# Attention and expert kernel: the transposed score blocks go to their partitions by way of DRAM

## The chip, the core and the metric

The kernel runs on one core of one Trainium2 chip. The metric is the device time of one execution in microseconds (us), the median of several runs. An engine is named as the profile names it: PE is TensorE (PEld its weight loads), DVE is VectorE, ACT is ScalarE, POOL is GpSimd, SP is SyncE, whose only work here is to issue DMA transfers.

## What is computed

Two blocks run one after the other, all in float32. The first is an attention without softmax over 8 batches of 2496 tokens; its output is multiplied with `u`. The second sends each token to one of 8 experts by a hash of its id and applies the two matrices of that expert.

```python
# u, v: (8, 2496, 256)   z: (8, 2496, 64)
scores = (1 / 2496) * z @ z.T                  # per batch, symmetric
x = u * (maximum(scores, 0) ** 2 @ v)          # (19968, 256) rows
expert = token_ids * 2654435761 % 8
for e in range(8):
    out[expert == e] = maximum(x[expert == e] @ w1[e], 0) @ w2[e]    # F = 1024
```

The scores are symmetric. What is computed for queries i and keys j serves, transposed, for queries j and keys i.

## The kernel before

**Tiles.** The 2496 tokens of a batch are 20 tiles: 19 of 128 tokens and a last one, number `TM` = 19, of 64 (`R`). Four tiles make a group (`G` = 4), five groups a batch (`NG` = 5); the last group has 448 queries, the others 512. A *block* is the 512 x 512 squared scores of one group of keys against one group of queries, kept in SBUF as four tiles `a` of 128 keys each. A 128 x 128 tile splits into *quarters* of 32 (`Q` = 32, `NQ` = 4).

**The order.** The whole program is written out by hand: the loops of Python emit the instructions, and every engine runs its own in the order in which they were emitted. The main loop goes over 40 pairs of batch and group (L651). For one group `g` of queries it runs

- `attend`: for each tile `t` of keys two matmuls (the even and the odd columns of `v`), weights from `v`, moving data the squares of that tile; sums over the tiles in two PSUM banks `acc`. Tiles of the group itself come last, the last three of them (`LATE`) only after the scores of the next group have been emitted;
- `attend_last` (L326): the short tile 19, as two pairs of matmuls of 64 rows each;
- `scores` for the next group (L203): matmuls of `z` against itself into six PSUM buffers, and a Relu into `a`, nearly always on ACT;
- after each step of `attend`: `square` (ACT, in place), `turn_scores` (transposes that are due), and `between` (L595), which counts the step `i`, fetches finished rows, and lets POOL scatter either one column of token numbers to DRAM (`enter`, L550, every fourth step in the middle of the attention) or 128 finished rows (`place_x`, L562).

**Which blocks are computed.** For group `g` only the blocks with keys in groups above `g` and the group's own block are computed (`fresh`). The blocks with keys below `g` are the transposes of earlier ones. They are kept in six buffers `mirror`. A batch has ten such blocks; four of them are made in group 0, three in group 1, two in group 2, one in group 3.

**Turning a block** (`turns_of`, L234). A block is turned in four turns, one for each quarter `c` of the queries. DVE transposes all 32 x 32 squares of that quarter from `a` into a buffer `stage` of 128 x 512 (L241); there are five such buffers (`spool`). The transposed data lie on partition quarters `r` by the key's place in its tile, but must get to the partition quarter `c`. Three of the four pieces go by DMA from SP (L251), 64 KB each in runs of 512 B; the one with `r == c` is already on its partitions and is copied by ACT (L249), in the next step. A `stage` is free again when these four have ended. `turn_now` forces what is still undone before a use. Some 1.2 turns are emitted in each step.

**The own block** (`own_turns`, L255): its lower half is filled in place by 32 to 48 small DVE transposes (L262), which stand behind the turns on DVE. The tiles of the own block that `LATE` uses need them.

**Rows of x** (`gate`, L334). DVE transposes each `acc` into `x_q` (L339, two buffers). Four transfers write it to DRAM (`x_way`, L346), and three steps later one or two read it back row by row into `x_sb` (L349, L351). POOL multiplies by `u` (L354), and the rows wait for `place_x`.

**Semaphores.** Every SP transfer waits on SP for what it needs, and nothing behind it on SP is issued until then.

After the attention come the expert blocks (`run`, L772), which take 512 or 128 tokens each. The change doesn't alter them, apart from the names of the dimensions of their buffers.

## Time and profile before

| what | value |
|---|---|
| median of 3 runs | 2682.76 us (2680.69 to 2684.29) |
| the profiled execution | 2685.0 us |
| its span, first to last instruction | 2683.3 us |
| granted PE clock, mean over the span | 0.996 of full speed |
| attention, up to the first expert matmul | 1560 us of the span |
| DVE: transposes into `stage` (L241) | 320, 218.0 us |
| DVE: transposes inside own blocks (L262) | 1408, 298.8 us |
| SP: transfers out of `stage` (L251) | 960 of 64 or 48 KB, 599 ns each in the median on SP |
| POOL: scatters of token numbers (L550) | 160, 156.3 us |
| all DMA | 357.21 MB, 133 GB/s in the mean |

The busy time of an engine is a sum over the span; the engines run side by side, so these sums don't add up to the span. A DMA that SP issues keeps SP busy only while it is being issued; the transfer itself runs on the DMA engines. The step of PE in a long run of equal matmuls is the distance of their starts, which is shorter than the length shown for one, as they overlap. A float32 matmul shows as two records.

### The profile page before, as it was taken

The numbers are of one execution on the slowest core, as the hardware profiler recorded it, in microseconds if no ns is written. First come the engines' busy times: TensorE is split into PE (matmuls) and PEld (weight loads), VectorE is DVE, ScalarE is ACT, GpSimd is POOL, SyncE is SP. The second block draws the span as 40 slices with busy tenths as digits, with TensorE's granted clock in tenths as the row PEclk, the third lists the DMA queues.
The fourth block names the chain that finished last, engine by engine and source line by source line (L and its number), as shares of the span: only waits on it lengthen the run. The fifth ranks groups of instructions, "written<-read, shape, count | busy, mean of one in ns | idle before, by whom it ended". The sixth has DMA issues, their size and how long they took to land. (4 is left out here: it accounts for less than half of the span.)

```text
span 2683.3 us, 28098 instructions
## 1 busy us (share of the span) xinstructions
PE 2652.4 (99%) x8854; PEld 1534.3 (57%) x8854; DVE 795.7 (30%) x2147; ACT 785.0 (29%) x1592; POOL 608.9 (23%) x671
## 2 busy tenths in 40 slices
PE   9999999999999999999999999999999999999999
PEld 5444444444444444444444457777777777777777
DVE  5634334434334333344344311111111111111110
ACT  7316326324334345245245101111111111111111
POOL 1331332233233233232321121111111111111112
PEclk9999999999999999999999999999999999999999
DMA  5544445545435534534534386666666666666663
GB/s 150 155 119 99 117 109 115 116 105 121 113 99 129 111 102 112 121 98 114 131 97 115 92 204 160 159 158 157 155 154 161 163 164 163 163 164 161 159 156 87
DMA packets 524247, 357.21 MB, mean 133 GB/s; under 512 B 277660, under 2 KB 487085, under 8 KB 524096
## 3 DMA queue, kind: packets, MB, share of 16 engines
q1 hardware_dynamic: 503360, 314.29, 50.1%
q0 software_dynamic: 20736, 41.09, 4.8%
q8 instruction: 72, 1.18, 0.2%
q14 instruction: 79, 0.65, 0.1%
HBM read 229.36 MB, written 67.53 MB: 111 GB/s over the span
## 5 line engine op out<-in xcount | busy, mean ns | idle before, releaser
L323 PE MATMUL acc<-a,v_sb 128*128 128x512 f32 (+1 forms) x1760 | 768.0, 593 | 0.0
L742 PE MATMUL h_ps<-v_sb,m 128*128 128x128 f32 (+1 forms) x2080 | 569.6, 432 | 3.0 <-DVE v_sb L644 1.9
L323 PEld LDWEIGHTS acc<-a,v_sb 128*128 128x128 f32 x1760 | 343.0, 197 | 391.6 <-issue 374.7
L754 PE MATMUL o_ps<-m,hT 128*128 128x256 f32 x2576 | 566.3, 379 | 0.0
L323 PE MATMUL acc<-m,v_sb 128*128 128x512 f32 (+1 forms) x1280 | 529.2, 571 | 5.5 <-DVE x_q L339 4.5
L754 PEld LDWEIGHTS o_ps<-m,hT 128*128 128x128 f32 x2576 | 487.0, 190 | 78.3 <-issue 15.0
L742 PEld LDWEIGHTS h_ps<-v_sb,m 128*128 128x128 f32 x2080 | 318.1, 191 | 238.0 <-issue 231.4
L323 PEld LDWEIGHTS acc<-m,v_sb 128*128 128x128 f32 x1280 | 250.5, 196 | 279.8 <-issue 267.7
L748 DVE TENSOR_SCALAR hT<-h_ps 128x512 f32<-128x512 f32 x161 | 111.4, 692 | 946.3 <-PE h_ps L742 540.6
L218 ACT ACTIVATE a<-s_ps 128x512 f32<-128x512 f32 (+3 forms) x456 | 203.6, 566 | 588.5 <-PE s_ps L210 439.6
L766 POOL DMA_INDIRECT out_dram<-o_sb,idx x157 | 153.6, 979 | 925.0 <-ACT o_sb L761 917.1
L354 POOL TENSOR_TENSOR x_sb<-x_sb,u_sb 128x256 f32<-128x256 f32 (+1 forms) x160 | 111.1, 723 | 989.0 <-DMA x_sb<-x_way 766.1
L262 DVE STREAM_TRANSPOSE a<-a 32x64 f32<-32x64 f32 (+3 forms) x1408 | 298.8, 241 | 20.0 <-ACT a L226 6.4
L249 ACT COPY m<-stage 32x512 f32<-32x512 f32 (+1 forms) x320 | 189.6, 593 | 300.9 <-DVE stage L241 139.7
L241 DVE STREAM_TRANSPOSE stage<-a 128x512 f32<-128x512 f32 x320 | 218.0, 700 | 200.8 <-DMA m<-stage 179.5
L226 ACT ACTIVATE a<-a 128x512 f32<-128x512 f32 (+1 forms) x480 | 236.9, 564 | 2.1
L761 ACT COPY o_sb<-o_ps 128x256 f32<-128x256 f32 x161 | 60.0, 372 | 596.6 <-PE o_ps L754 596.6
L210 PE MATMUL s_ps<-zT 64*128 64x512 f32 (+2 forms) x960 | 207.6, 555 | 16.7 <-ACT a L218 11.3
L339 DVE STREAM_TRANSPOSE x_q<-acc 128x512 f32<-128x512 f32 (+1 forms) x80 | 56.4, 705 | 552.1 <-PE acc L323 501.5
L746 ACT ACTIVATE hT<-h_ps 128x512 f32<-128x512 f32 x161 | 96.1, 597 | 398.9 <-PE h_ps L742 390.7
L210 PEld LDWEIGHTS s_ps<-zT 64*128 64x128 f32 x960 | 118.4, 192 | 123.0 <-issue 75.6
L562 POOL DMA_INDIRECT x_rows<-x_sb,slot_i x160 | 157.7, 986 | 43.2 <-issue 37.2
(93 smaller groups left out, 390.2 us busy)
## 6 DMA issues: line engine op xcount, KB each, us to landing
m<-in_moe_w_dram SPq DMA_DIRECT2D x260, 256.0 KB
m<-in_moe_w_dram SPq DMA_DIRECT2D x65, 1024.0 KB
m<-stage SPq DMA_DIRECT2D x768, 64.0 KB
v_sb<-in_v_dram SPq DMA_DIRECT2D x32, 512.0 KB
u_sb<-in_u_dram SPq DMA_DIRECT2D x32, 512.0 KB
x_way<-x_q SPq DMA_DIRECT2D x128, 128.0 KB
x_sb<-x_way SPq DMA_DIRECT2D x32, 512.0 KB
v_sb<-x_rows SPq DMA_DIRECT2D x128, 128.0 KB
```

The costliest lines, as they stand in the source:

```text
L210: nc.tensor.matmul(ps[:, lo:n], zT[b][h, ts(t, P)], zT[b][h, ds(g * G * P + lo, n - lo)], start=True, stop=True)
L218: nc.scalar.activation(a, ps[:, lo:n], AF.Relu)
L226: nc.scalar.activation(a, a, AF.Square, scale=1.0 / S)
L241: nc.vector.transpose(stage[:].rearrange("p (n q) -> p n q", q=Q), made[key][:].rearrange("p t (s q) -> p (t s) q", q=P)[:, :, ts(c, Q)])
L249: to_copy.append((key, lambda o=o, x=x: nc.scalar.copy(o, x)))
L262: return lambda: nc.vector.transpose(out, in_)
L323: nc.tensor.matmul(acc[h][:, 0:queries(g)], v_sb[b][:, t, h::2], squares(b, g, t), start=(k == 0), stop=(k == TM - 1), skip_group_check=True)
L562: st = nc.gpsimd.indirect_dma_start(out=x_dram[:, :], out_offset=bass.IndirectOffsetOnAxis(ap=slot_i[0:width(c % T), c:c + 1], axis=0), in ...
L742: nc.tensor.matmul(ps[:, ts(i, n)], w1[j][:, c, ts(k * m + i, P)], xT[j][:, :, c, :], start=(c == 0), stop=(c == DP - 1))
L748: nc.vector.tensor_scalar_max(o, ps[:], 0.0)
L754: nc.tensor.matmul(ps[:], hT[j][f][:, ts(t, P)], w2[j][:, f, :], start=(f == 0), stop=(f == FP - 1))
L766: st = nc.gpsimd.indirect_dma_start(out=out[:], out_offset=bass.IndirectOffsetOnAxis(ap=rows, axis=0), in_=o, in_offset=None, bounds_check ...
```

## The change

`stage` is written to DRAM whole, in one transfer a turn, and when all four turns of a block have been written, one transfer reads the block back into its `mirror`. The DRAM tensor `way` has the quarter and the partition in it as its first two dimensions, so the read is 128 rows of 8 KB. There are four such tensors, taken in turn. The read is put into the list `to_fetch` and is issued two steps after the block's last turn, or at once where the block is used earlier. The list `to_copy` and its ACT copies are gone.

The dimensions of `mirror` are now (quarter r, tile i, source tile s, query q) in place of (i, r, s, q), and the columns of `acc` follow: quarter first, then tile. In the last group two of the four quarters have four tiles and two have three, so `squares` gives two parts there, of 256 and 192 columns, and each matmul of that group becomes two. `x_way` has its rows in this order too, and its read is four transfers, one for each quarter of the partitions. The blocks read directly (`a`) are read in runs of 32 columns. `spool` has six buffers for five, `qpool` one for two.

```diff
-    qpool = pool("qpool", 2)
-    spool = pool("spool", 5)
+    qpool = pool("qpool", 1)
+    spool = pool("spool", 6)
...
+    way = [nc.dram_tensor(f"way_{k}", (NQ, Q, NQ, G * G * Q), F32) for k in range(4)]
...
             nc.vector.transpose(stage[:].rearrange("p (n q) -> p n q", q=Q),
                                 made[key][:].rearrange("p t (s q) -> p (t s) q", q=P)[:, :, ts(c, Q)])
-            for r in range(NQ):
-
-                m = len(group(g)) if r * Q < width(group(g)[-1]) else G - 1
-                o = mirror[key][ts(c, Q), 0:m, r].rearrange("p i s q -> p i (s q)")
-                x = stage[ts(r, Q), 0:m * G * Q].rearrange("p (i n) -> p i n", i=m)
-                if r == c:
-                    to_copy.append((key, lambda o=o, x=x: nc.scalar.copy(o, x)))
-                else:
-                    nc.sync.dma_start(o, x)
+            nc.sync.dma_start(ways[key][c].rearrange("j r x -> r j x"), stage[:])
+            if c == NQ - 1:
+                to_fetch.append((i + 2, key, lambda: nc.sync.dma_start(
+                    mirror[key][:].rearrange("p r i s q -> p (r i s q)"), ways[key][:].rearrange("c j r x -> (c j) (r x)"))))
...
         if t in fresh(b, g):
-            a = made[b, g, t // G][:, t % G, :].rearrange("p (n q) -> p n q", q=Q)
+            a = made[b, g, t // G][:, t % G, :].rearrange("p (i r q) -> p r i q", r=NQ, q=Q)
         else:
-            a = mirror[b, t // G, g][:].rearrange("p i r s q -> p s (i r) q")[:, t % G]
-        return a[:, 0:queries(g) // Q]
+            a = mirror[b, t // G, g][:, :, :, t % G, :]
+        parts, c = [], 0
+        for r in ([slice(0, NQ)] if TM not in group(g) else [slice(0, R // Q), slice(R // Q, NQ)]):
+            m = G if r.start < R // Q else G - 1
+            n = (r.stop - r.start) * m * Q
+            parts.append((slice(c, c + n), a[:, r, 0:m]))
+            c += n
+        return parts
...
         for h in halves:
-            nc.tensor.matmul(acc[h][:, 0:queries(g)], v_sb[b][:, t, h::2], squares(b, g, t),
-                             start=(k == 0), stop=(k == TM - 1), skip_group_check=True)
+            for cols, a in squares(b, g, t):
+                nc.tensor.matmul(acc[h][:, cols], v_sb[b][:, t, h::2], a,
+                                 start=(k == 0 and cols.start == 0), stop=(k == TM - 1), skip_group_check=True)
...
-        def fetch():
-            nc.sync.dma_start(xs[:, 0:m], o[0:m].rearrange("i j p d -> (j p) i d"))
-            if m < G:
-                nc.sync.dma_start(xs[0:R, m], o[m, 0:R // Q].rearrange("j p d -> (j p) d"))
+        def rows_of_x():
+            c = 0
+            for r in range(NQ):
+                m = G if r * Q < width(group(g)[-1]) else G - 1
+                nc.sync.dma_start(xs[ts(r, Q), 0:m], o[c:c + m].rearrange("i p d -> p i d"))
+                c += m
...
-        if to_fetch and to_fetch[0][0] <= i:
-            to_fetch.pop(0)[1]()
+        fetch(lambda e: e[0] <= i)
```

More of the change, by code (lines that the diff above doesn't have):

```diff
@@ L81 @@
     xpool = pool("xpool", 3)
-    qpool = pool("qpool", 2)
-    spool = pool("spool", 5)
+    qpool = pool("qpool", 1)
+    spool = pool("spool", 6)
     x_dram = nc.dram_tensor("x_rows", (NS * P, D), F32)
-    x_way = [nc.dram_tensor(f"x_way_{k}", (G, NQ, Q, D), F32) for k in range(2)]
+    way = [nc.dram_tensor(f"way_{k}", (NQ, Q, NQ, G * G * Q), F32) for k in range(4)]
+    x_way = [nc.dram_tensor(f"x_way_{k}", (G * NQ, Q, D), F32) for k in range(2)]
     slot_dram = nc.dram_tensor("slot_tokens", (P * NS,), I32)
@@ L122 @@
     uf, vf, zf = (x.rearrange("b s d -> (b s) d") for x in (u, v, z))
-    zn, zT, v_sb, u_sb, x_q, made, mirror, to_square, to_turn, to_fetch, gated = {}, {}, {}, {}, {}, {}, {}, [], [], [], []
+    zn, zT, v_sb, u_sb, x_q, made, mirror, ways, to_square, to_turn, to_fetch, gated = {}, {}, {}, {}, {}, {}, {}, {}, [], [], [], []
     def load_z(b):
@@ L239, in turn @@
                 mirror[key] = mirrors.pop(0)
+                ways[key] = way[len(ways) % len(way)]
             stage = spool.tile([P, G * G * Q], F32, name="stage")
@@ L275, in own_turns @@
                         yield move(tiles[ds(h * R + c * Q, Q), 3, 0:3, ts(r, Q)], tiles[i, 0:3, 3, ts(c, Q)])
-    to_copy = []
     share = 0
@@ L282, in turn_scores @@
         nonlocal share
-        copy_turned(to_copy[:])
         share += 1.2 * steps
@@ L296, in turn, with fetch @@
         e[1]()
-    def copy_turned(those):
-        for e in those:
-            to_copy.remove(e)
-            e[1]()
+    def fetch(due):
+        for e in [e for e in to_fetch if due(e)]:
+            to_fetch.remove(e)
+            e[2]()
     def turn_now(key):
@@ L305, in turn_now @@
             turn(e)
-        copy_turned([e for e in to_copy if e[0] == key])
+        fetch(lambda e: e[1] == key)
     def squares(b, g, t):
         if t in fresh(b, g):
-            a = made[b, g, t // G][:, t % G, :].rearrange("p (n q) -> p n q", q=Q)
+            a = made[b, g, t // G][:, t % G, :].rearrange("p (i r q) -> p r i q", r=NQ, q=Q)
         else:
-            a = mirror[b, t // G, g][:].rearrange("p i r s q -> p s (i r) q")[:, t % G]
-        return a[:, 0:queries(g) // Q]
+            a = mirror[b, t // G, g][:, :, :, t % G, :]
[6 more added lines that the diff above has]
+        return parts
     def attend(b, g, k, acc, halves):
@@ L322, in attend @@
         for h in halves:
-            nc.tensor.matmul(acc[h][:, 0:queries(g)], v_sb[b][:, t, h::2], squares(b, g, t),
-                             start=(k == 0), stop=(k == TM - 1), skip_group_check=True)
+            for cols, a in squares(b, g, t):
+                nc.tensor.matmul(acc[h][:, cols], v_sb[b][:, t, h::2], a,
+                                 start=(k == 0 and cols.start == 0), stop=(k == TM - 1), skip_group_check=True)
     def attend_last(b, g, acc):
         turn_now((b, TM // G, g))
-        for h in range(2):
-            rows = ds(h * R, R)
-            nc.tensor.matmul(acc[h][:, 0:queries(g)], v_sb[b][rows, TM, h::2], squares(b, g, TM)[rows],
-                             start=False, stop=False, skip_group_check=True)
+        for cols, a in squares(b, g, TM):
+            for h in range(2):
+                rows = ds(h * R, R)
+                nc.tensor.matmul(acc[h][:, cols], v_sb[b][rows, TM, h::2], a[rows],
+                                 start=False, stop=False, skip_group_check=True)
     def gate(b, g, h, acc):
@@ L345, in gate @@
         for a in range(NQ):
-            nc.sync.dma_start(o[:].rearrange("i j p d -> p (i j) d")[:, 0:n, ts(a, D // NQ)], x[ts(a, Q), 0:n])
-        m = len(whole(g))
-        def fetch():
-            nc.sync.dma_start(xs[:, 0:m], o[0:m].rearrange("i j p d -> (j p) i d"))
-            if m < G:
-                nc.sync.dma_start(xs[0:R, m], o[m, 0:R // Q].rearrange("j p d -> (j p) d"))
+            nc.sync.dma_start(o[:].rearrange("n p d -> p n d")[:, 0:n, ts(a, D // NQ)], x[ts(a, Q), 0:n])
+        def rows_of_x():
[4 more added lines that the diff above has]
+                c += m
             for k, t in enumerate(group(g)):
@@ L355, in fetch @@
                 gated.append((b * T + t, y))
-        to_fetch.append((i + 3, fetch))
+        to_fetch.append((i + 3, None, rows_of_x))
     idx = const.tile([P, NS], I32)
@@ L407, in places @@
             total, rank = counts[:, 0], counts[:, 1]
-            room = sorting[:].rearrange("p i r s q -> p (i r s q)")
+            room = sorting[:].rearrange("p r i s q -> p (r i s q)")
             upto = room[:, 0:E * C].rearrange("p (e c) -> p e c", e=E)
@@ L629, in load_w @@
     def load_w(j, k):
-        w1[j] = w_buf[2 * k][:].rearrange("p i r s q -> p (i r s q)").rearrange("p (h f) -> p h f", h=DP)
-        w2[j] = w_buf[2 * k + 1][:].rearrange("p i r s q -> p (i r s q)").rearrange("p (c d) -> p c d", c=FP)
+        w1[j] = w_buf[2 * k][:].rearrange("p r i s q -> p (r i s q)").rearrange("p (h f) -> p h f", h=DP)
+        w2[j] = w_buf[2 * k + 1][:].rearrange("p r i s q -> p (r i s q)").rearrange("p (c d) -> p c d", c=FP)
         e = nc.sync.value_load(eb_i[0:1, j:j + 1], min_val=0, max_val=E - 1)
@@ L646 @@
     mpool = pool("mirror", 1)
-    mirrors = [mpool.tile([P, G, NQ, G, Q], F32, name=f"m_{k}") for k in range(NG * NG // 4)]
+    mirrors = [mpool.tile([P, NQ, G, G, Q], F32, name=f"m_{k}") for k in range(NG * NG // 4)]
     sorting = mirrors.pop()
@@ L714 @@
     assert not to_turn and next(place, None) is None and i > SORT + 4 * C
-    for _, f in to_fetch:
-        f()
+    fetch(lambda e: True)
     while gated:
```

## The prediction, made before the changed kernel had run

> **What bounds the kernel now.** I read the page's busy shares first, then the timeline of TensorE at the seams between query groups, then SP, DVE and POOL at one of these seams, then the DMA queues.

> ```profile
> PE 2652.4 (99%) x8854; PEld 1534.3 (57%) x8854; DVE 795.7 (30%) x2147; ACT 785.0 (29%) x1592; POOL 608.9 (23%) x671
> ...
> L249 ACT COPY m<-stage 32x512 f32<-32x512 f32 (+1 forms) x320 | 189.6, 593 | 300.9 <-DVE stage L241 139.7
> ```

> TensorE is busy for 99% of the span. ScalarE is not the bound, so the 189.6 us of copies that go (L249) are worth only what they hold up. Work of TensorE that is added costs its whole length; a stall of TensorE costs its whole length too.

> The timeline shows where it is not fed. Call A0 to A4 the attention stages of one batch's five groups and S1 the scores between A0 and A1 (L331 and L210). Batch 1 first, then batch 7, the last:

> ```profile
> 237.12 1.14 PE L331 MATMUL acc<-a,v_sb 64*128 64x512 f32 x4
> 238.09 2.74 PE L210 MATMUL s_ps<-zT 64*128 64x512 f32 x12
> 242.88 5.86 PE L210 MATMUL s_ps<-zT 64*128 64x512 f32 x20 [2.05 <-ACT a L218]
> 248.68 1.56 PE L323 MATMUL acc<-a,v_sb 128*128 128x512 f32 x3
> ...
> 1407.70 1.14 PE L331 MATMUL acc<-a,v_sb 64*128 64x512 f32 x4
> 1408.67 6.60 PE L210 MATMUL s_ps<-zT 64*128 64x512 f32 x32
> 1415.20 1.13 PE L323 MATMUL acc<-a,v_sb 128*128 128x512 f32 x2
> ```

> From L331 to the next L323, S1 takes 11.6 us in batch 1 and 7.5 in batch 7. Summed over the eight batches, S1 is 23.9 us above 7.5 each, and S2 (5.6 at best) 11.9 above: 36 us, the only sizable slack. The other stages repeat to 0.1 us, but for 7.5 us in all at the starts of A4.

> ```profile
> 237.62 0.98 POOL L550 DMA_INDIRECT slot_tokens<-token,addr  x1 [0.30 <-issue]
> 238.91 0.98 POOL L550 DMA_INDIRECT slot_tokens<-token,addr  x1 [0.30 <-issue]
> ...
> 213.48 7.81 SPq L251 DMA_DIRECT2D m<-stage  x12
> 221.46 0.46 SPq L349 DMA_DIRECT2D x_sb<-x_way  x1
> ...
> 216.93 0.71 DVE L241 STREAM_TRANSPOSE stage<-a 128x512 f32<-128x512 f32 x1 [3.52 <-DMA m<-stage]
> ...
> 236.71 3.80 DVE L262 STREAM_TRANSPOSE a<-a 32x64 f32<-32x64 f32 x17
> ```

> The slow S1 and S2 are those in which POOL's token scatters (L550) run into the scores; batch 7 has none and no stall. They come in a burst after x_sb lands, and x_sb is late because its fetch (L349) queues on SP behind turns at 1.95 us each (three transfers). DVE is paced by the same transfers: it waits for a free `stage`, and its last turns of the own block (L262 x17) end at 240.5, before A1 needs them (A0 began at 204.9, so A1 could begin at 244.6). That leaves DVE about 4 us of room.

> [...] Every SP transfer of the kernel before in this stage has 32, 64 or 128 rows outermost[...]. [...] SP's longest wait for `x_way` is 2.8 us. [...] the granted clock falls to a half for 3.4 us after the 2.05 us stall above (the mean of that stretch is 0.96), and so I count 1.7 us for each long stall.

> **The change part by part.**

> *Matmuls of the last group.* 304 matmuls of 448 columns (L323; two records each, 608) become 256 + 192, and 16 pairs of half height (L331) become 32.

> ```profile
> 1530.35 24.22 PE L323 MATMUL acc<-m,v_sb 128*128 128x448 f32 x64
> ...
> 1573.81 13.98 PE L754 MATMUL o_ps<-m,hT 128*128 128x256 f32 x64
> 1587.62 3.73 PE L742 MATMUL h_ps<-v_sb,m 128*128 128x128 f32 x32
> ```

> A run of n is n-1 steps and one length (541, 379 and 275 ns), so a step is 376 ns for 448 columns, 216 for 256, 111.5 for 128; 192 lie between the last two, 164. So 380 against 376: 608 x 4 ns = 2.4 us. A half-height pair costs some 0.1 us beyond its columns, 16 more pairs 1.7 us. Together +4 us. If the weight load (197 ns) bound the 192 columns it would be 608 x 33 = 20 us more; the row of 128 columns at 111.5 ns with a load each excludes that. Reading `a` in runs of 32 costs nothing: L323 on `m` does so already and takes 592 ns against 596.

> *ScalarE copies.* 320 copies go, 189.6 us off an engine that TensorE seldom waits for. Nothing by itself.

> *SP.* A turn issues one transfer instead of three (1.95 us to some 0.6), plus a quarter of a read; the `x_sb` fetch has four issues instead of one or two (+0.8 us). By itself this brings x_sb and L550 forward by about 6 us and takes them out of S1 and S2: up to -36 us.

> *The write of a turn.* Its target is `ways[key][c].rearrange("j r x -> r j x")`: the slowest dimension is r, of 4. The source has 128 partitions. [...] 64 KB on each of four DMA engines[...]. This is the step that decides. How long 64 KB take on one engine is not in the trace; two bounds. [...] Above, the rate of the stores that the trace has:

> ```profile
> q0 software_dynamic: 20736, 41.09, 4.8%
> ```

> 4.8% of 16 x 2683.3 us for 41.09 MB is 19.9 GB/s, 3.3 us. I take 2.9. [...]

> *What it does to DVE.* There are now 6 `stage` buffers, so turn n waits until turn n-6 has landed. The 16 turns of A0 and 12 of A1 come at 1.5 us each and are served at 2.9 plus the rest. Load of these four engines from the start of A0 until the last turn of A1 (the 28th, freed by the 22nd) may start, estimates from packet counts at the queue's rates: 22 writes x 2.9 = 63.8; 5 mirror reads of 1 MB, 64 KB an engine, 2.6 each = 13; the rows through `x_way` twice, write 2.3 and read 1.3, = 7.2; u and the scattered rows 2.8. Sum 86.8. Add 5 until the first turn is there (208.35 + 0.71 against 204.9), 2.6 where SP waits for the writes of the last key and has nothing else in the rings[...]: 96.4. Then the turn and some 20 own turns behind it, 5.6: DVE is done at 102.0. TensorE needs that block at the start of A2, without stalls at 39.7 (A0 and S1: 32.2 + 7.5) + 38.4 (A1 and S2: 32.8 + 5.6) = 78.1. So 24 us of stall a batch, some 7 of them already at A1 (10 writes: DVE done at 46.7 against 39.7). A2 has 8 turns and A3 4, so the queue drains there and in A4: 40 writes x 2.9 = 116 us and 10 reads = 26 fit into 193 us a batch, so nothing carries over. 8 x 24 = 192 us.

> *The reads into the mirrors.* SP waits for the landing of four writes; behind it stand the next turns' writes and the x_sb fetch. Their consumers are 15 or more steps of 1.7 us away, so TensorE does not wait for a mirror itself.

> *x_q with one buffer.* Its next use is 35 us later. Nothing. *End of attention:* +1 us, the chain x_way, x_sb, scatter, load to the first expert blocks.

> Sum: 2685.0 (the profiled execution; its span 2683.3) + 192 + 16 stalls x 1.7 = 27 for the clock + 4 + 1 - 36 = 2873. The first batch has less to move (no rows of a batch before, some 4 us), and the median of the runs is 2 us lower: **2865**.

> **The rivals.**
> *B, the writes spread over all 16 engines (faster).* Then a write is 0.7 us, DVE is never late, SP's load falls, and the 36 us of S1 and S2 go but for 2 or 3: 2682.8 - 34 + 5 = **2654**. For it: the stall stands and falls with L550. Against: the outermost dimension of 4. It decides if writes land in under some 1.7 us.
> *C, four engines, but fast.* [...] 2685 + 88 + 20 + 5 - 36 = 2762, **2760**.
> *D, spread, and the stall of S1 and S2 stays* because L550 only meets other loads: only +5, **2688**, no gain. The L331 to L323 times would show it.
> That the copies might not really go is no rival: L249 is gone from the program.

> **How the numbers follow.** Forecast A 0.62, C 0.20, B 0.14, D 0.04. A's own range is 2790 (2.5 us a write) to 2960 (3.3 us: 9 more a batch). The range 2690 to 2960 leaves out B, D and A's upper tail, under 2 in 10. A measurement here can tell about 0.2%, 5 us. Faster: B, 0.14. Same: part of D, 0.02. Slower: 0.84.

> **What would show it.** Right: DVE's L241 waiting for `way<-stage` in A0 and A1, by 2.5 to 3.3 us a turn; TensorE waiting at the starts of A1 and A2 on DVE's L259 (the own turns), 7 and 17 us; more half-clock stretches; L323 of 256 and 192 columns stepping at 216 and 164. Wrong: turns at 1.5 us with `stage` free, S1 at 7.5 us in every batch, a span near 2655.

## The result, and the profile after

| | kernel before | changed kernel |
|---|---|---|
| median | 2681.73 us (2679.57 to 2684.29, 4 runs) | 2864.2 us (2857.06 to 2878.41, 4 runs) |
| ratio | | 1.0693, 95% interval 1.0673 to 1.0713 |
| profiled execution, span | 2685.0, 2683.3 us | 2857.06, 2855.4 us |
| granted PE clock, mean | 0.996 | 0.972 |
| attention, up to the first expert matmul | 1560 us | 1732 us |

The change made the kernel 6.9% slower; the forecast was 2865 us. The profile of the changed kernel first, its busy shares and three of the groups (busy us and mean ns of one, then idle time before them and what ended most of it); the last line is the transposes into `stage` in the kernel before:

```profile
PE 2688.1 (94%) x9494; PEld 1646.0 (58%) x9494; DVE 791.5 (28%) x2147; ACT 588.5 (21%) x1272; POOL 609.0 (21%) x671
...
L327 PE MATMUL acc<-a,v_sb 128*128 128x512 f32 (+2 forms) x1856 | 805.6, 592 | 124.8 <-DVE a L259 100.7
...
L327 PE MATMUL acc<-m,v_sb 128*128 128x512 f32 (+2 forms) x1792 | 534.7, 458 | 18.4 <-DMA m<-way 13.7
...
L243 DVE STREAM_TRANSPOSE stage<-a 128x512 f32<-128x512 f32 x320 | 219.3, 701 | 520.6 <-DMA way<-stage 493.5
...
L241 DVE STREAM_TRANSPOSE stage<-a 128x512 f32<-128x512 f32 x320 | 218.0, 700 | 200.8 <-DMA m<-stage 179.5
```

ACT is rid of its copies (785.0 to 588.5 us of busy time), and PE has fallen from 99% to 94% of the span. The third group and the first are one chain: DVE waits 493.5 us for a `stage` whose write hasn't landed (179.5 us for the three transfers of before); its own-block transposes (L259), which stand behind the turns, come late; TensorE waits 100.7 us for them. The second group is a wait that the prediction had excluded: TensorE waits 13.7 us for a mirror.

The timeline of PE shows the two seams of batch 3, S1 from the first L336 and S2 from the second (the first line is the start of A0; the bracket is the idle time before the line and what ended it):

```profile
666.25 6.53 PE L327 MATMUL acc<-a,v_sb 128*128 128x256 f32 x28
...
700.15 1.14 PE L336 MATMUL acc<-a,v_sb 64*128 64x512 f32 x4
701.12 6.17 PE L211 MATMUL s_ps<-zT 64*128 64x512 f32 x26
...
714.46 7.61 PE L327 MATMUL acc<-a,v_sb 128*128 128x512 f32 x12 [3.34 <-DVE a L259]
...
749.47 1.14 PE L336 MATMUL acc<-a,v_sb 64*128 64x512 f32 x4
750.44 4.68 PE L211 MATMUL s_ps<-zT 64*128 64x512 f32 x24
763.49 4.85 PE L327 MATMUL acc<-a,v_sb 128*128 128x512 f32 x7 [8.38 <-DVE a L259]
```

S1 takes 14.3 us against the 7.5 of an undisturbed one, S2 14.0 against 5.6. DVE in the same stretch:

```profile
674.07 3.63 DVE L243 STREAM_TRANSPOSE stage<-a 128x512 f32<-128x512 f32 x6
683.78 0.71 DVE L243 STREAM_TRANSPOSE stage<-a 128x512 f32<-128x512 f32 x1 [6.08 <-DMA way<-stage]
686.38 0.71 DVE L243 STREAM_TRANSPOSE stage<-a 128x512 f32<-128x512 f32 x1 [1.89 <-DMA way<-stage]
688.92 0.71 DVE L243 STREAM_TRANSPOSE stage<-a 128x512 f32<-128x512 f32 x1 [1.83 <-DMA way<-stage]
...
758.26 0.71 DVE L243 STREAM_TRANSPOSE stage<-a 128x512 f32<-128x512 f32 x1 [3.23 <-DMA way<-stage]
759.00 4.43 DVE L259 STREAM_TRANSPOSE a<-a 32x128 f32<-32x128 f32 x20
```

Six turns fill the six buffers within 3.6 us. From then on a turn starts when a write has landed, at best 2.6 us after the one before it (686.38 - 683.78, 688.92 - 686.38), though it takes 0.71; up to 758.26, with the reads of blocks and the rows of x between the writes, it is 3.7 us in the mean of 20. The last own turn ends at 763.43, and TensorE goes on at 763.49.

For all the kernels below I took the same measure from the timeline of PE: the length of each stage in every batch, from the first L327 (L323 before) to L336 (L331) for A0 to A4 and from there to the next L327 for the scores, less the shortest length that any of the kernels shows for it (A0 32.2, S1 7.5, A1 to A3 32.8, S2 5.6, S3 3.9, S4 2.0, A4 29.4, the scores after A4 8.9; the A0 of batch 0, which is shorter, counts as 0). Sums over eight batches, us:

| kernel | A0 | S1 | A1 | S2 | A2 | S3, A3 | from A4 | all |
|---|---|---|---|---|---|---|---|---|
| before | 0 | 23.9 | 0 | 11.9 | 2.1 | 0.4 | 7.4 | 45.7 |
| changed | 19.7 | 56.1 | 17.2 | 61.6 | 15.4 | 20.9 | 20.3 | 211.2 |
| e1, four writes | 0 | 8.6 | 0 | 1.1 | 2.5 | 0.4 | 11.4 | 24.0 |
| e2, two engines | 21.1 | 255.1 | 15.9 | 294.4 | 17.8 | 199.1 | 193.8 | 997.1 |
| e3, rows outermost | 0 | 0 | 0 | 0 | 0 | 0 | 3.9 | 3.9 |
| e4, before, scatters moved | 0 | 0.7 | 0 | 0 | 0 | 0.5 | 26.5 | 27.7 |
| e5, changed, pools of before | 19.3 | 81.7 | 18.3 | 76.6 | 18.8 | 10.6 | 3.5 | 228.8 |
| e6, changed, scatters moved | 0 | 61.8 | 19.5 | 59.9 | 16.5 | 18.8 | 101.6 | 278.1 |
| e7, changed, five stages | 0 | 90.0 | 16.3 | 78.1 | 18.7 | 12.2 | 2.0 | 217.3 |

What the changed kernel lost lies in the attention: 211.2 - 45.7 = 165.5 us; from there to the end it takes 7.5 us more (1135.3 for 1127.8), as the first expert matmul waits 7.4 us for its rows of x (DVE, L649). Together 173.0 us, against 172.1 between the spans.

### The profile page after: what moved, and what is told of

It is laid out like the page before. It is cut to its first block, busy times and chain, and to the rows that moved or that the text cites. A ratio compares the mean times of both kernels' runs of the same rounds, so it can differ in the third digit from the quotient of the medians.

```text
span 2855.4 us, 28325 instructions
## 1 busy us (share of the span) xinstructions
PE 2688.1 (94%) x9494; PEld 1646.0 (58%) x9494; DVE 791.5 (28%) x2147; ACT 588.5 (21%) x1272; POOL 609.0 (21%) x671
## 3 DMA queue, kind: packets, MB, share of 16 engines
q0 software_dynamic: 20736, 41.09, 5.1%
## 5 line engine op out<-in xcount | busy, mean ns | idle before, releaser
L327 PE MATMUL acc<-a,v_sb 128*128 128x512 f32 (+2 forms) x1856 | 805.6, 592 | 124.8 <-DVE a L259 100.7
L327 PEld LDWEIGHTS acc<-a,v_sb 128*128 128x128 f32 x1856 | 370.8, 204 | 527.5 <-issue 394.1
L327 PE MATMUL acc<-m,v_sb 128*128 128x512 f32 (+2 forms) x1792 | 534.7, 458 | 18.4 <-DMA m<-way 13.7
L758 PEld LDWEIGHTS o_ps<-m,hT 128*128 128x128 f32 x2576 | 487.0, 190 | 78.1 <-issue 14.8
L327 PEld LDWEIGHTS acc<-m,v_sb 128*128 128x128 f32 x1792 | 337.1, 198 | 215.6 <-issue 179.2
L243 DVE STREAM_TRANSPOSE stage<-a 128x512 f32<-128x512 f32 x320 | 219.3, 701 | 520.6 <-DMA way<-stage 493.5
L360 POOL TENSOR_TENSOR x_sb<-x_sb,u_sb 128x256 f32<-128x256 f32 (+1 forms) x160 | 111.5, 727 | 1148.5 <-DMA x_sb<-x_way 1069.7
L259 DVE STREAM_TRANSPOSE a<-a 32x64 f32<-32x64 f32 (+3 forms) x1408 | 298.2, 241 | 14.2 <-ACT a L227 0.2
L227 ACT ACTIVATE a<-a 128x512 f32<-128x512 f32 (+1 forms) x480 | 227.9, 615 | 0.0
L211 PE MATMUL s_ps<-zT 64*128 64x512 f32 (+2 forms) x960 | 198.6, 538 | 8.5 <-issue 6.5
L556 POOL DMA_INDIRECT slot_tokens<-token,addr x160 | 156.3, 977 | 48.6 <-issue 48.6
```

The lines of the kernel that those rows point to most:

```text
L211: nc.tensor.matmul(ps[:, lo:n], zT[b][h, ts(t, P)], zT[b][h, ds(g * G * P + lo, n - lo)], start=True, stop=True)
L227: nc.scalar.activation(a, a, AF.Square, scale=1.0 / S)
L243: nc.vector.transpose(stage[:].rearrange("p (n q) -> p n q", q=Q), made[key][:].rearrange("p t (s q) -> p (t s) q", q=P)[:, :, ts(c, Q)])
L259: return lambda: nc.vector.transpose(out, in_)
L327: nc.tensor.matmul(acc[h][:, cols], v_sb[b][:, t, h::2], a, start=(k == 0 and cols.start == 0), stop=(k == TM - 1), skip_group_check=True)
L360: nc.gpsimd.tensor_mul(y, y, u_sb[b, g][0:width(t), k, :])
```

## The experiments

Measured again beside e1 to e6, the kernel before took 2677 to 2678 us.

### The four engines: e1, e2, e3

The write of a turn has r, of 4, as the slowest dimension of its target. e1 cuts it into four writes with 32 rows outermost; nothing else changes.

```diff
-            nc.sync.dma_start(ways[key][c].rearrange("j r x -> r j x"), stage[:])
+            for r in range(NQ):
+                nc.sync.dma_start(ways[key][c][:, r], stage[ts(r, Q)])
```

> Undoes one thing of the changed kernel: a turn is written by four transfers of 32 rows each in place of one whose outermost dimension is 4. Same bytes, same rows of 2 KB, same tensor, same read. The theory (the write ran on 4 DMA engines, 2.7 us a turn, and DVE waited for stage): [...] DVE's wait for stage falls from 493 us to under 200, the waits of TensorE for the own turns (100.7 us) are gone, and SP's four issues a turn (some 2 us) set the pace as in the kernel before: 2660 to 2720 us. The rival (the detour through DRAM itself, its volume and landing time): 2830 us or more.

Measured: 2661.82 us (2656.86 to 2665.37), ratio 0.9939 (0.9922 to 0.9957). Same bytes, same buffers, same rows of 2 KB, and the loss is gone. In its view of waits DVE still waits for `stage`, 224.5 us where under 200 were expected, but TensorE no longer for DVE (us in total, times, longest):

```profile
DVE stage L243 <- DMA way<-stage: 224.5, 120, 7.7
...
PE acc L328 <- DVE a L260: 0.7, 1, 0.7
```

e2 goes the other way: two writes a turn, each with two rows outermost.

```diff
-            nc.sync.dma_start(ways[key][c].rearrange("j r x -> r j x"), stage[:])
+            for h in range(2):
+                nc.sync.dma_start(ways[key][c][:, ts(h, 2)].rearrange("j r x -> r j x"), stage[ts(h, R)])
```

> The suspected cost doubled: a turn is written by two transfers whose outermost dimension is 2, [...] 128 KB an engine and turn, 64 rows of 2 KB at 84 ns = 5.4 us a turn. Same bytes. The theory: 40 turns x 5.4 = 215 us, with the mirror reads (26) and the rest (some 25) 266 us a batch on these two engines against 193 us of work: about 8 x 70 = 560 us over the kernel before, 3150 to 3400 us. The rival (volume or landing time): two transfers in place of one change little, 2840 to 2900 us.

Measured: 3647.66 us (3644.97 to 3656.24), ratio 1.3634 (1.361 to 1.3659). The direction is the theory's, the size is more than it gave: the time is outside the range expected. DVE's timeline, with the buffers full:

```profile
358.49 0.71 DVE L243 STREAM_TRANSPOSE stage<-a 128x512 f32<-128x512 f32 x1 [4.47 <-DMA way<-stage]
363.61 0.71 DVE L243 STREAM_TRANSPOSE stage<-a 128x512 f32<-128x512 f32 x1 [4.41 <-DMA way<-stage]
...
368.75 0.71 DVE L243 STREAM_TRANSPOSE stage<-a 128x512 f32<-128x512 f32 x1 [3.81 <-DMA way<-stage]
```

5.1 us a turn, twice the 2.6 with four rows outermost. The packets in the traces point to two DMA engines for a write of two rows and four for one of four. In the attention of these kernels the packets of 2 KB are those of the writes alone (128 a turn, 40960 in the changed kernel). While any is under way there are 2.0 at once in the mean in e2 (at most three for 99.8% of that time), 3.3 in the changed kernel (at most five for 99.5%), and 8.5 in e1. A packet took 84 ns in the median in the changed kernel, so the 128 of a turn would take 2.7 us four at a time and 5.4 two at a time, an estimate beside the 2.6 and 5.1 measured. On which engine a packet ran the traces don't show: "four engines" and "two engines" stand for these counts.

Why e2 lost 970 us and not the 560 of its expectation is shown in part. The expectation had counted that the queue doesn't drain (266 us of load for 193 us of work a batch), but a batch now takes 314 us in the mean. It had not counted that the mirrors come late too:

```profile
PE acc L328 <- DVE a L260: 512.9, 16, 40.1
PE acc L328 <- issue: 216.4, 9, 39.6
PE acc L328 <- DMA m<-way: 166.4, 8, 22.9
```

e3 keeps one write a turn and turns `way` around, so that the write has 128 rows outermost and the permutation is done by the reads, one for each quarter of the partitions.

```diff
-    way = [nc.dram_tensor(f"way_{k}", (NQ, Q, NQ, G * G * Q), F32) for k in range(4)]
+    way = [nc.dram_tensor(f"way_{k}", (NQ, NQ, Q, G * G * Q), F32) for k in range(4)]
...
-            nc.sync.dma_start(ways[key][c].rearrange("j r x -> r j x"), stage[:])
+            nc.sync.dma_start(ways[key][c].rearrange("r j x -> (r j) x"), stage[:])
...
-                to_fetch.append((i + 2, key, lambda: nc.sync.dma_start(
-                    mirror[key][:].rearrange("p r i s q -> p (r i s q)"), ways[key][:].rearrange("c j r x -> (c j) (r x)"))))
+                to_fetch.append((i + 2, key, lambda: [nc.sync.dma_start(
+                    mirror[key][ts(k, Q)].rearrange("p r i s q -> p r (i s q)"), ways[key][k].rearrange("r j x -> j r x")) for k in range(NQ)]))
```

> The changed kernel with the way tensor as (c, r, j, x): a turn is written by one transfer of 128 rows, and a block is read back by four of 32 partitions with rows of 2 KB. [...] Same bytes; 8 issues a block on SP for 5. The theory: no wait of DVE of note; SP's load is below that of the kernel before, the x rows come some 6 us earlier, the token scatters leave S1 and S2, which take 7.5 and 5.6 us: 2645 to 2670 us. If the scatters' overlap was not what held S1 and S2 up: about 2690. The rival (the detour itself): 2800 or more.

Measured: 2642.24 us (2638.59 to 2642.57), ratio 0.9866 (0.9849 to 0.9882): 1.3% faster than the kernel before, 3 us below the range expected. DVE's wait for `stage` is down to 71.6 us. Its busy shares and the seam of batch 1 in its timeline:

```profile
PE 2630.8 (100%) x9494; PEld 1630.4 (62%) x9494; DVE 790.9 (30%) x2147; ACT 584.8 (22%) x1272; POOL 608.1 (23%) x671
```

```profile
235.41 1.14 PE L336 MATMUL acc<-a,v_sb 64*128 64x512 f32 x4
236.38 6.60 PE L211 MATMUL s_ps<-zT 64*128 64x512 f32 x32
242.91 2.42 PE L327 MATMUL acc<-a,v_sb 128*128 128x512 f32 x5
```

7.5 us, without a gap, and so in all eight batches. POOL's burst of token scatters in this batch ends at 234.5, before S1 begins. In e1, where a turn issues four writes on SP for one, three scatters still fall at batch 1's S1, which takes 1.9 us longer there.

### The scatters: e4, e6

e4 is the kernel before with the token scatters (L550) in groups 2, 3 and 4 alone, so that none can run into S1 and S2.

```diff
-        elif i % 4 == 0 and i < SORT + 4 * C:
+        elif entered < C and (i % 3 < 2 if i // 20 % 5 == 3 else i // 20 % 5 > 1 and i % 4 == 0):
...
-            enter((i - SORT) // 4)
+            enter(entered)
+            entered += 1
```

> The kernel before with one thing moved: the scatters of token numbers (L550) are emitted in the groups 2, 3 and 4 alone, so that none runs in S1 or S2. If these scatters are what holds S1 and S2 up: S1 is 7.5 and S2 5.6 us in every batch, 36 us less, 2640 to 2655 us. If SP's backlog of turns or the loads of u and v do it: S1 and S2 unchanged, 2675 to 2690 us.

Measured: 2663.87 us (2659.08 to 2664.47), ratio 0.9945 (0.9928 to 0.9961). S1 and S2 fall from 35.8 us to 0.7, so the scatters are what these stages lost: in the kernel before 12 of them start in S1 and 19 in S2, none here. (The scatters of finished rows, L562, take the steps that are left and shift a little, but none starts in S1 or S2 in either kernel.) But A4, where many of them now are, rises from 7.4 to 26.5, and the time misses the range expected. The cost moved with its cause. PE and DVE in one such A4 (POOL issues scatters, nearly all L550, at a step of 1.28 us up to 942.3):

```profile
938.80 21.54 PE L323 MATMUL acc<-m,v_sb 128*128 128x448 f32 x49 [3.18 <-DVE x_q L339]
...
938.03 0.72 DVE L339 STREAM_TRANSPOSE x_q<-acc 128x512 f32<-128x512 f32 x1 [3.73 <-remote]
938.78 3.02 DVE L262 STREAM_TRANSPOSE a<-a 32x96 f32<-32x96 f32 x16
942.19 0.27 DVE L262 STREAM_TRANSPOSE a<-a 32x96 f32<-32x96 f32 x1 [0.39 <-issue]
943.59 0.33 DVE L262 STREAM_TRANSPOSE a<-a 32x64 f32<-32x64 f32 x2 [1.13 <-DMA x_way<-x_q]
945.00 0.33 DVE L262 STREAM_TRANSPOSE a<-a 32x64 f32<-32x64 f32 x2 [1.08 <-issue]
```

TensorE loses 3.18 us because DVE, which frees its `acc`, starts late at 938.03. Later small transposes that otherwise run 0.2 us apart start only every 1.40 us for a while, mostly with nothing that the profile could name as their releaser. (The wait for `x_way<-x_q` at 943.59 can't be told from this: it ends at the same step.)

e6 makes the same edit in the changed kernel.

> The changed kernel with POOL's token scatters (L550) in groups 2, 3 and 4 only, as in e4_scatters_moved. Theory (the 20 us that the starts of A0 lost in the changed kernel belong to the scatters, which come there by way of the late x_sb; the waits of S1 and S2 belong to the four-engine writes): A0's excess falls below 5 us, S1 and S2 keep 90 us or more, A4 rises by up to 20; 2845 to 2870 us. Rival 1 (A0's excess belongs to the four-engine queue): A0's stays at 15 to 20 us. Rival 2 (the waits at S1 and S2 are the scatters' too): S1 and S2 fall by half or more, below 2800 us.

Measured: 2922.14 us (2915.4 to 2924.45), ratio 1.0909 (1.0885 to 1.0932). A0's 19.7 us go to 0: they were the scatters'. S1 and S2 keep 121.7 us against 117.7: these are the writes'. Both rivals fall. The time is outside the range expected, since from A4 on 101.6 us are lost where up to 40 were expected: the last mirror is late there (below), and on top of it PE starts single matmuls at the same step of 1.40 us:

```profile
442.27 0.38 PE L327 MATMUL acc<-m,v_sb 128*128 128x256 f32 x1 [1.35 <-issue]
443.67 0.32 PE L327 MATMUL acc<-m,v_sb 128*128 128x192 f32 x1 [1.02 <-issue]
445.08 0.32 PE L327 MATMUL acc<-m,v_sb 128*128 128x192 f32 x1 [1.09 <-issue]
...
448.58 0.79 PE L327 MATMUL acc<-m,v_sb 128*128 128x256 f32 x1 [0.82 <-issue]
449.98 0.68 PE L327 MATMUL acc<-m,v_sb 128*128 128x192 f32 x1 [0.61 <-issue]
```

The clock takes its part as well: in this A4, from 418.63 to 460.15, its mean is 0.88, some 5 us of the 12 lost there.

### The waits at A4: e5, e7

In the changed kernel TensorE waits for a mirror in A4. SP and PE in batch 1:

```profile
396.12 0.33 SPq L247 DMA_DIRECT2D m<-way  x1
...
399.25 2.60 SPq L147 DMA_DIRECT2D zn<-in_z_dram  x1
...
412.86 1.73 SPq L356 DMA_DIRECT2D x_sb<-x_way  x4
414.69 3.07 SPq L245 DMA_DIRECT2D way<-stage  x4
417.81 2.64 SPq L121 DMA_DIRECT2D v_sb<-in_v_dram  x1
432.09 0.70 SPq L247 DMA_DIRECT2D m<-way  x1
```

```profile
415.58 18.32 PE L327 MATMUL acc<-m,v_sb 128*128 128x256 f32 x96
437.33 2.98 PE L327 MATMUL acc<-m,v_sb 128*128 128x256 f32 x14 [3.43 <-DMA m<-way]
```

The four writes of the batch's last block are issued only at 414.69, though DVE had turned it by 388.2. SP stood until 396.12 for the landing that the read of the block before waits for, and from 399.25 to 412.7 it issued the loads of `z` for the next batch, then the fetch of `x_sb`. After the four writes it stands until they have landed, to 432.09, before it issues the read, and the mirror is there 5 us later, 3.4 us after TensorE wanted it. e5 asks whether the pools have a share in it: it gives `x_q` its second buffer back and, for lack of room, takes the sixth `stage` away.

```diff
-    qpool = pool("qpool", 1)
-    spool = pool("spool", 6)
+    qpool = pool("qpool", 2)
+    spool = pool("spool", 5)
```

> The changed kernel with the pools of before: stage in five buffers, x_q in two. Theory (the four-engine queue sets the end of DVE's turns, and x_q with one buffer costs nothing): one more write, 2.7 us, must have landed before the last turn of A1 starts, so 8 x 2.7 = 22 us longer than the changed kernel, 2870 to 2900 us; the starts of A0 and A4 keep their waits, 20 us each in the sum over the batches. Rival (the waits at A0 and A4 that were not predicted come from x_q's one buffer, which lets DVE reach the own turns late): these 40 us go and the time falls to 2830 to 2850 us in spite of the buffer lost.

Measured: 2865.79 us (2862.41 to 2870.08), ratio 1.0699 (1.068 to 1.0718). Neither came out. S1 and S2 lose 40.6 us more, 5 a batch where I had put 2.7, and A4 loses 16.8 less, as the rival had it; the whole is the same as the changed kernel's within the intervals. e7 takes only the sixth `stage` away (`spool` 5, `x_q` one).

> The changed kernel with stage in five buffers and x_q in one: it differs from e5_pools_back by x_q alone, from the changed kernel by one stage. Theory (x_q with one buffer costs nothing; the buffer of stage lost moves the stall from A4 to S1 and S2, as in e5_pools_back): A0 to S2 lose 190 to 200 us over the clean lengths, as in e5_pools_back (196), A4 3 to 6, 2860 to 2875 us. Rival (x_q's one buffer is what made A4 wait in the changed kernel, 20 us): A4 loses 15 to 25 us here too and the time is 2880 us or more.

Measured: 2854.82 us (2854.66 to 2859.54), 5 us below the range expected. From A4 on it loses 2.0 us with one `x_q`, so the rival falls, as far as kernels on two chips can be compared: a single `x_q` by itself does not make A4 wait. What the buffer of `stage` does is to shift the wait: in batch 1 of e5 SP issues the four writes at 414.91, within 0.3 us of the changed kernel, but A4 begins at 413.89 instead of 410.31, since TensorE has waited longer before, and so the mirror is in time. A0 to S2 lose 184 us, 6 short of the range expected, with nothing lost in A0. Beside e7, on another chip, the kernel before took 2638.3 us (2637.67 to 2639.39), 40 us less than in all others, so that its ratio of 1.0827 (1.0808 to 1.0845) can't be set beside e5's.

### The same kernels on one chip: e8 to e11

The 2638 us raise a question about e3: is its gain worth anything on that chip? Four kernels were run again, unchanged.

> The kernel before, unchanged. In the call of e7_five_stages it took 2638.3 us, in those of e1 to e6 2677 to 2678. Theory: the 40 us between them are its waits in S1 and S2 (36 us in the profile of before), that is, how much the token scatters hold up differs from chip to chip; the rest is the same on all. Then the tally of its stages gives 0 to 10 us above the clean lengths where it takes about 2638, and 36 to 46 where it takes about 2678. Rival: the chip is faster throughout (clean stages shorter by 1.5%, A1 at 32.3 us for 32.82).

> The changed kernel, unchanged, on the chip of this call. Theory: the stall in S1 and S2 belongs to the four-engine writes and doesn't depend on the chip: A0 to S2 lose 140 to 160 us, 2835 to 2870 us whatever the kernel before takes; where the kernel before takes 2638, A0 alone loses nothing. Rival: it keeps its ratio of 1.069 to the kernel before, 2820 us where that takes 2638.

> e3_rows_outermost, unchanged, on the chip of this call. Theory (it is within 4 us of the clean stage lengths already): 2637 to 2645 us on any chip. So where the kernel before takes 2638 us it is no faster, ratio 1.000 to 1.003; where that takes 2678, 0.985 to 0.989. Rival: the gain is of the copies and transfers saved and holds on any chip: ratio 0.987 in both cases.

> e5_pools_back, unchanged, on the chip of this call, to be read against e9 (one stage more, one x_q less) and, if the chip is that of e7, against e7_five_stages (x_q alone). Theory: the end of DVE's turns is set by the four engines: A0 to S2 lose 185 to 200 us here against 140 to 160 in e9, A4 0 to 5 against 10 to 20; x_q's second buffer is worth less than 8 us. Rival: x_q's second buffer is worth 15 us or more (2840 us or less where e7 took 2855).

Measured, with the kernel before at 2677.63 us beside them: before 2677.37 us (ratio 1.0003, 0.999 to 1.0016), changed 2861.02 (1.0683, 1.0654 to 1.0711), rows outermost 2642.36 (0.9865, 0.9848 to 0.9882), pools of before 2865.67 (1.07, 1.0681 to 1.0719). The stages of e8 lose 41.4 us in all, 33.9 of them in S1 and S2, those of e10 2.3. So e3's gain is repeated, but this was not the chip of e7. What can be said of that one: it is not faster throughout, since the undisturbed stages of e7 are as long as those of e5 (A0 32.21, A3 32.82, A4 29.57 us in both). A0 of e7 lost nothing, where A0 of e5 lost 19.3 and of e11 21.7, as if scatters cost less on it. The profiled kernel before, 2683.3 us, would take 2637.6 without the 45.7 us of the table, about what it took there; and e3's 2642 us on other chips are no less. So e3 would probably gain nothing on that chip. This is not shown: neither e3 nor a profile of the kernel before was taken on it.

e9 beside e11 confirms e5: A0 to S2 lose 151.6 and 196.3 us, from A4 on 26.2 (10 to 20 were expected) and 3.6, and the times are 4.7 us apart. The effect of `x_q` alone was not measured on one chip.

## Why the prediction was right

The mechanism was right. That the total is within 1 us (2865 for 2864.2) is luck: the terms erred in both directions, and the last step of the sum, 2873 less 4 and less 2, gives 2867. On the profiled executions: predicted 192 + 27 + 4 + 1 - 36 = +188. Measured, from the table: 154.6 (A0 to S2) + 15.4 (A2) + 20.9 (S3, A3) + 20.3 (from A4) + 7.5 (start of the experts) - 45.7 (what the kernel before lost) = +173.

- **The write of a turn: right.** That an outermost dimension of 4 means four engines was my assumption; no trace of before showed it. The packets of the changed kernel agree with it (3.3 at once in the mean, at most five for 99.5% of the time), and so do the steps of 2.6 us there and 5.1 in e2. The 2.9 us of a write measured 2.6 (DVE's step; a 2 KB packet took 84 ns in the median, and 32 x 84 = 2.7 us are 64 KB).
- **The stall of DVE: right, 24 us a batch measured 19.3** (A0 to S2, 154.6 us over eight batches, against 192; 17.7 a batch where no scatters add to it, e6). In the batch shown above DVE is done 763.43 - 666.25 = 97.2 us after the start of A0, where I had 102.0 against TensorE's 78.1. A write shorter by 0.3 us is enough for that (22 x 0.3 = 6.6); the other terms were not measured one by one. The 96.4 us of the prediction hold an allowance for the last landing that no trace of before showed by itself; for SP's transfers there is one number here, with the transfer in it: POOL starts on its rows of x at 660.55, 2.6 us after SP has issued the last of their four reads. S1 waits 7.0 us a batch in the mean (7 predicted), S2 7.7 (17 predicted), because the rest of DVE's lateness had been used up before: by A0's own waits and by the half clock of A1.
- **The clock: mis-sized by counting twice.** 16 stalls x 1.7 = 27 us were added. After S2 that is right in size (A2 15.4 us for 8 x 1.7 = 13.6), and it is the clock: in batch 3 A1 takes 35.01 us at a mean clock of 0.94 and A2 34.39 at 0.95, without a gap in either. In A1 17.2 us are lost too, but they are inside the 19.3: as long as DVE is late for S2 anyway, a slow A1 costs nothing. One reading was too quick: the 1.7 us come from a single stretch of 3.4 us at half clock, after a stall of 2.05 us in the kernel before. In the changed kernel such stretches last 3.4 to 13.7 us, 6.8 from 712.09 and from 759.88 in batch 3; what sets one off, and what decides its length, is not shown.
- **S1 and S2 without the scatters, -36 us: right in the sum, not in the way.** The scatters did not leave: 26 token scatters start in S1 of the changed kernel and 6 in S2, for 12 and 19 before. They still delay the scores: in batch 3 the wait for L259 is 3.34 of the 6.8 us that S1 loses, the rest lies in the scores before it. But they add nothing to the sum, since DVE is late in these stages anyway (without them, e6, S1 and S2 lose 121.7 us for 117.7), and so the old 36 us are not on top of the new stall. e3 shows the step as it was meant: no scatter starts in S1 or S2, and both are at their shortest in all batches. The cause named, scatters that run into the scores, is shown by e4. That they can cost elsewhere was left out: 5 or 6 now fall in A0 in most batches (3 before), and A0 lost 19.7 us in all; without them there (e6) A0 to S2 lost 13.4 us less. (That the other stages of before "repeat to 0.1 us" overlooked 2.1 us in A2 of batch 5 and 0.4 in S3 of batch 0.)
- **The mirrors: wrong.** "TensorE does not wait for a mirror itself" and "nothing carries over" left out that the writes of a batch's last block are issued late, behind a wait of SP and the loads of `z`, and that SP stands until they have landed. From A4 on 20.3 us were lost against 7.4. Not foreseen either: batch 0 loses 12.8 us in S3, where TensorE waits for DVE's own turns and not for a mirror, and DVE had stood 13.07 us for a `stage` (up to 138.60), although the queue was to drain by then.
- **The split matmuls: right in sign, smaller.** Steps of 216 and 163 ns for the predicted 216 and 164; the shortest A4 went from 29.41 to 29.57 us, 1.3 us over eight batches for the 4 predicted.
- **ScalarE's copies, worth nothing by themselves:** not tried alone. e4 has all of them and loses 1.2 us up to A3, so they hold up next to nothing there.
- **x_q with one buffer:** not shown to cost anything, not measured alone. **End of attention:** +7.5 us for +1; with the pools of e5 it was +1.2 (1129.0). What makes the difference is open.

The rivals: B (the writes spread, 2654 us) described what e1 and e3 then did, 2662 and 2642. C, four engines but a faster write, rested on a write time that no trace showed; the 154.6 us lost in A0 to S2, where it had 88, exclude it. D, the old stall of S1 and S2 in spite of spread writes, is excluded by e3.

## What to carry to other kernels

Look at the slowest dimension of a transfer's target, and not only at the length of its rows: the same 256 KB took 5.1 or 2.6 us with 2 or 4 rows outermost, and with 128 no time that TensorE waited for; and the permutation, which was needed, could be put on the other side of the way through DRAM. A pool between a producer and a DMA frees a buffer when the transfer lands (DVE waited 493.5 us for that in the changed kernel), so sum the load of the busiest DMA engines up to each deadline, and the waits of the issuing queue with it; a `stage` less, with an `x_q` more, cost 41 us more in S1 and S2, 27 less from S3 on, and changed the total by at most 5. Where an off-path engine's burst costs time, moving it may only move the cost (A4 of e4 lost 26.5 us for 7.4).
